# Gated mix of one-token attention and a feed-forward layer: loads of K and V in two halves, from SyncE and GpSimd

## The chip, the cores and the metric

The kernel runs on one core of a Trainium2 chip. The core has engines that work side by side: PE (TensorE) multiplies matrices, DVE (VectorE) and ACT (ScalarE) work on elements, POOL (GpSimd) and SP (SyncE) are here used to issue transfers or not at all. Sixteen DMA engines move data between HBM, the large memory, and SBUF, the core's own memory of 128 partitions. Any engine that issues a DMA puts it in a queue of its own; the same sixteen DMA engines serve all queues. Engines wait for each other through semaphores, which are counters: a DMA adds 16 when it has landed.

The metric is the device time of one execution in microseconds (us), lower being better. Each kernel is run several times.

## The reference

```python
def _A_ref(x, k_cache, v_cache, wq, wo):        # x [1,1,512], caches [1,32,65536,128]
    q = (x @ wq) as [B, H, Sq, Dh]               # 32 heads of 128
    scores = einsum("bhqd,bhkd->bhqk", q, k_cache) * (Dh ** -0.5)
    p = _softmax(scores, axis=-1)
    o = einsum("bhqk,bhkd->bhqd", p, v_cache)
    return o as [B, Sq, H * Dh] @ wo
def _B_ref(x, w_gate, w_up, w_down):             # 512 -> 1792 -> 512
    return (_silu(x @ w_gate) * (x @ w_up)) @ w_down
g = _sigmoid((x * gate_w).sum(-1, keepdims=True))
return g * a + (1 - g) * b
```

(The reshapes of q and o are told in words here.) One token attends to 65536 cached tokens in each of 32 heads. K and V are bf16: 65536 x 128 x 2 bytes, 16.8 MB each per head, 1.07 GB in all. Every byte is used once.

## The kernel before, in words

**Loads.** K and V of a head come in two halves of the tokens each, z = 0 (`a`) and z = 1 (`z`). In one half a partition holds 256 neighbouring tokens, so its piece of HBM is one run of 256 x 128 x 2 bytes = 64 KB, and the load is 8.389 MB. This is one DMA (L223 to L225). All of them are issued by SyncE, in the order written in L226 to L249: K of the next head, V of this one, in turn. The very first half of K is issued in two parts of 32 KB per partition (L228), so that work starts early. Behind the loop SyncE issues the weights wo and the last half of V in shrinking pieces (L250 to L261).

**Buffers.** `mem` has 184 KB per partition. K's two halves lie at KB 32 to 96 and 0 to 64, V's at 120 to 184 and 96 to 160. They overlap, so a load can go out when the part that it overwrites has been used, and not before. This is what SyncE's waits say: it waits for `ktdone`, which DVE counts up for each transposed eighth of a half of K, and for `pvdone`, which PE counts up four times a head in the product with V.

- the next head's first half of K is issued after four of eight transposes of this head's second half, and the second half after four transposes of the first;
- V's second half goes out after the product has used the first 40 of 64 groups of rows of V's first half, and the next head's first half after the first 40 groups of the second.

So there is never more than one load of K and one of V that has been issued and not used in part.

**Work on K.** DVE transposes K in eighths (L415 for the first half, L422 for the second; L322 for head 0) into two buffers `kt` in turn. PE multiplies each with q (`scores`, L472, 32 matmuls for an eighth) and counts `qkdone`. DVE may be no more than two eighths ahead.

**Work on V.** In head i PE also does the product of head i-1's probabilities with V (`values`, L525): `values(0, 0)` after six eighths of K's first half, `values(0, 1)` after all eight, `values(1, 0)` after the second half, `values(1, 1)` behind the maximum of the scores. Parts 0 have 40 matmuls, parts 1 have 24. PE runs this order as written; a wait of one step holds up all behind it. Before `values(0, 0)` PE waits for `d["va"]`, before `values(1, 0)` for `d["vz"]`; DVE waits for `d["ka"]` in L407 and `d["kz"]` in L418 before the transposes of a half. Each of these semaphores stands for one buffer's loads.

GpSimd writes four constants at the start and has nothing else to do.

Of the kernel before, what the change touches and what calls it, by code (L numbers as in the profile page):

```python
# [21 lines left out]
def bass_gated_mix__mha_block_cached__swiglu_ffn__decode_kernel(  # L22
# [13 lines left out]
    _, H, S, Dh = A_k_cache.shape  # L36
# [5 lines left out]
    HR = R // 2  # L42
    NP = HR // PR
# [21 lines left out]
    with ExitStack() as ctx:  # L65
# [6 lines left out]
        def sem(name):  # L72
            return ctx.enter_context(nc.semaphore(name))
# [35 lines left out]
        def at(kb, n):  # L109
            return mem[:, kb * KB:kb * KB + n]  # L110
# [9 lines left out]

        names = ("x", "gw", "wq", "wg", "wu", "wd", "ka0", "ka", "kz", "va", "vz", "wo", "wj", "w31")
        d = {n: sem("d_" + n) for n in names}
        dt_ = [sem(f"d_t{i}") for i in range(len(tail))]
        s_ones = sem("s_ones")
        s_sel0 = sem("s_sel0")
# [75 lines left out]
        def place(kind, h, z):  # L201
            if kind == "k":
                return (KA, V0)[z] if isinstance(h, int) and h == 0 else (KA, KZ)[z]
            return (VA, VZ)[z]
# [12 lines left out]
        ctx.callback(lambda: nc.sync.wait_ge(s_out2, 16))  # L217
        block = ctx.enter_context(nc.Block())

        @block.sync  # L220
        def _(sp):
            def load(kind, h, z):
                cache = A_k_cache if kind == "k" else A_v_cache  # L223
                sp.dma_start(at(place(kind, h, z), HR * Dh), kv_dram(cache, h)[z]).then_inc(d[kind + "az"[z]], 16)  # L224

            half = HR // 2 * Dh  # L226
            for n in range(2):
                sp.dma_start(at(KA + 32 * n, half), kv_dram(A_k_cache, 0)[0][:, n * half:n * half + half]).then_inc(  # L228
                    (d["ka0"], d["ka"])[n], 16)
            sp.wait_ge(s_q, 1)  # L230
            load("k", 0, 1)
            sp.wait_ge(ktdone, NP)
            load("k", 1, 0)
            sp.wait_ge(ktdone, 2 * NP - 3)
            sp.wait_ge(s_b, 1)
            load("v", 0, 0)
            sp.wait_ge(ktdone, 2 * NP + NP // 2)
            load("k", 1, 1)
            sp.wait_ge(pvdone, 5)
            load("v", 0, 1)  # L240
            with nc.sync.Fori(0, H - 2) as i:
                sp.wait_ge(ktdone, i * (2 * NP) + (4 * NP - 4))
                load("k", i + 2, 0)
                sp.wait_ge(pvdone, i * 4 + 7)
                load("v", i + 1, 0)
                sp.wait_ge(ktdone, i * (2 * NP) + (4 * NP + NP // 2))
                load("k", i + 2, 1)
                sp.wait_ge(pvdone, i * 4 + 9)
                load("v", i + 1, 1)  # L249
            sp.wait_ge(ktdone, 2 * NP * H - NP)  # L250
            sp.dma_start(at(WO, 31 * D), w_dram["wo"][:, 0:31 * D]).then_inc(d["wo"], 16)
            src = A_v_cache[0, H - 1].rearrange("(b p r) d -> b p (r d)", b=2, p=P)
            need = {0: (ktdone, 2 * NP * H - 4), 1: (ktdone, 2 * NP * H), 2: (pvdone, 4 * H - 1)}
            for n, (kb, r0, nr) in enumerate(tail):
                if n in need:
                    sp.wait_ge(*need[n])
                b, o = divmod(r0, HR)
                sp.dma_start(at(kb, nr * Dh), src[b][:, o * Dh:(o + nr) * Dh]).then_inc(dt_[n], 16)
            sp.wait_ge(pvdone, 4 * H)
            sp.dma_start(at(WOJ, D), wj_dram).then_inc(d["wj"], 16)  # L260
            sp.dma_start(at(WO31, D), w31_dram).then_inc(d["w31"], 16)  # L261
            sp.wait_ge(s_fin, 1)
            sp.dma_start(out_dram[2:4, :], fin[32:34, :]).then_inc(s_out2, 16)
# [41 lines left out]
        def _(dve):  # L305
# [6 lines left out]

            def transposes(z):
                dve.wait_ge(d[("ka0", "kz")[z]], 16)
                for c, u in enumerate(k_order[z]):
                    i = NP * z + c
                    if i == NP // 2:
                        dve.wait_ge(d["ka"], 16)
                    if i >= 2:
                        dve.wait_ge(qkdone, i - 1)  # L320
                    src = at(place("k", 0, z) + 8 * u, PR * Dh).bitcast(U32)
                    nc.vector.transpose(kt[:, i % 2, :].rearrange("p (j r t) -> p r j t", j=2, t=32),  # L322
                                        src.rearrange("p (r j t) -> p r j t", j=2, t=32)).then_inc(ktdone, 1)
# [79 lines left out]
            with nc.vector.Fori(1, H) as i:  # L403
                n = i * (2 * NP)
                v = i * 4
                dma = i * 16
                dve.wait_ge(d["ka"], dma + 16)  # L407
                for c, u in enumerate(k_order[0]):
                    if c == NP // 2:
                        dve.wait_ge(expdone, i)  # L410
                        dve.wait_ge(pvdone, v - 2)
                        shuffle(0, s_pba)
                    dve.wait_ge(qkdone, n + (c - 1))
                    src = at(KA + 8 * u, PR * Dh).bitcast(U32)
                    nc.vector.transpose(kt[:, c % 2, :].rearrange("p (j r t) -> p r j t", j=2, t=32),  # L415
                                        src.rearrange("p (r j t) -> p r j t", j=2, t=32)).then_inc(ktdone, 1)
                late(v, i, i)
                dve.wait_ge(d["kz"], dma + 16)  # L418
                for c, u in enumerate(k_order[1]):
                    dve.wait_ge(qkdone, n + (NP + c - 1))  # L420
                    src = at(KZ + 8 * u, PR * Dh).bitcast(U32)
                    nc.vector.transpose(kt[:, c % 2, :].rearrange("p (j r t) -> p r j t", j=2, t=32),  # L422
                                        src.rearrange("p (r j t) -> p r j t", j=2, t=32)).then_inc(ktdone, 1)
                top(i, n + 2 * NP)
# [20 lines left out]
        def _(pe):  # L445
# [58 lines left out]
            with nc.tensor.Fori(0, H) as i:  # L504
                n = i * (2 * NP)

                def pair(c, j):
                    for b in range(2):
                        if c == 0 and b == 0:
                            pe.wait_ge(s_qc, i + 1)  # L510
                        pe.wait_ge(ktdone, n + (c + b + 1) if j is None else n + j * 2 + (c + b + 1))
                        scores(b, PR * c, j)

                def pieces(z, c0, c1):
                    if c1 - c0 == 2:
                        pair(NP * z + c0, None)
                        return
                    with nc.tensor.Fori(0, (c1 - c0) // 2) as j:
                        pair(NP * z + c0, j)

                def values(z, part):
                    rows = v_order[z][part]
                    vt = at((VA, VZ)[z], HR * Dh)
                    for m, r in enumerate(rows):
                        last = nc.tensor.matmul(psO[0:4, :], pb[:, k_col[256 * z + r]:k_col[256 * z + r] + 4],  # L525
                                                vt[:, r * Dh:(r + 4) * Dh],
                                                start=(z == 0 and part == 0 and m == 0),
                                                stop=(z == 1 and part == 1 and m == len(rows) - 1))
                    last.then_inc(pvdone, 1)

                pieces(0, 0, NP - 2)
                with nc.tensor.If(i > 0):
                    pe.wait_ge(s_or, i)
                    pe.wait_ge(d["va"], i * 16)
                    pe.wait_ge(s_pba, i)
                    values(0, 0)
                pieces(0, NP - 2, NP)
                with nc.tensor.If(i > 0):
                    turn()
                    values(0, 1)  # L540
                pieces(1, 0, NP)
                with nc.tensor.If(i > 0):
                    pe.wait_ge(d["vz"], i * 16)
                    pe.wait_ge(s_pbz, i)
                    values(1, 0)
                pe.wait_ge(s_mx, i + 1)
                nc.tensor.matmul(mrow, mxs, ident[:], start=True, stop=True).then_inc(s_mt, 1)  # L547
                pe.wait_ge(s_gm, i + 1)
                nc.tensor.matmul(amx, onesf[0:1, :], gm, start=True, stop=True).then_inc(s_ar, 1)  # L549
                with nc.tensor.If(i > 0):  # L550
                    values(1, 1)
                pe.wait_ge(expdone, i + 1)
                nc.tensor.matmul(Lt, onesf[:], rsum, start=True, stop=True).then_inc(s_L, 1)  # L553
# [77 lines left out]
```

## Time and profile before

| | |
|---|---|
| time, median of 3 runs | 2514.06 us (2513.88 to 2514.1) |
| span of the profiled execution | 2512.4 us |
| HBM read in it | 1087.77 MB |
| PE, DVE, ACT, POOL busy | 68%, 56%, 3%, 0% of the span |
| chain that ended last | DMA 70%, PE 27% |

The profile is one execution, recorded by the hardware. "Busy" counts the time in which an engine ran an instruction; issuing a DMA isn't counted. The slices show busy time along the span in 40 equal parts of 62.8 us. The groups name line, engine and operation, then out<-in, the number of instructions, their busy time and mean, and the idle time before them with what ended it. The chain of waits goes back from the last instruction to what released it each time. For a DMA issue, "us to landing" is the time from its issue to the arrival of all its data, and it includes the time behind other loads. In the order of time, a row that merges several instructions of a line has its start, its length and their number; SPq, ACTq and the like are the engines' issuing side.

### The profile page before, as it was taken

What the parts mean: (1) busy time and instruction counts of PE and PEld (TensorE: products, weight loads), DVE (VectorE), ACT (ScalarE), POOL (GpSimd) and SP (SyncE); (2) the same over time, 40 slices, a digit from 0 to 9 for tenths busy, and PEclk for the clock granted to TensorE, in tenths of its full rate; (3) what the DMA queues carried; (4) which work ended last, traced back from release to release, by engine and by line L of the source; (5) the groups of instructions that cost most, each with busy time, mean ns of one, the idle gap of its engine ahead of it and who ended that gap; (6) DMA issues with size and microseconds to landing.
All of it is one profiled execution on the core that took longest, in us unless ns stands there. A gap on an engine that the chain in (4) does not pass through costs nothing.

```text
span 2512.4 us, 51694 instructions
## 1 busy us (share of the span) xinstructions
PE 1709.8 (68%) x21624; PEld 978.8 (39%) x21624; DVE 1411.8 (56%) x1683; ACT 64.6 (3%) x195; POOL 0.2 (0%) x4
## 2 busy tenths in 40 slices
PE   4666766667667677676676766766767767677677
PEld 3334433333433344333443333343334333344334
DVE  4764565554655645646456555465564564645653
ACT  0000000000000000000000000000000000000000
POOL 0000000000000000000000000000000000000000
PEclk8667767777677677776776767767767677677677
DMA  9999999999999999999999999999999999999999
GB/s 420 436 434 434 434 435 434 434 434 434 434 434 434 434 434 434 434 434 434 434 434 434 434 434 434 434 434 434 434 434 434 434 434 434 435 434 434 434 435 402
DMA packets 20470, 1087.93 MB, mean 433 GB/s; under 512 B 2282, under 2 KB 2668, under 8 KB 2924
## 3 DMA queue, kind: packets, MB, share of 16 engines
q1 hardware_dynamic: 20452, 1087.78, 100.0%
q8 instruction: 9, 0.15, 0.0%
q14 instruction: 1, 0.01, 0.0%
q10 hardware_dynamic: 8, 0.00, 0.0%
HBM read 1087.77 MB, written 0.00 MB: 433 GB/s over the span
## 4 chain that ended last, share of the span: by engine, by line
DMA 70%; PE 27%; DVE 1%; issue 1%; SPq 0%; ACT 0%; DVEq 0%
DMA mem<-in_A_v_cache_dram 67%; PE psO L525 27%; DMA mem<-in_A_k_cache_dram 2%; DMA mem<-in_A_wo_dram 1%; DVE kt L322 1%; DMA mem<-in_A_wq_dram 0%; DVE kt L415 0%; SPq L224 0%; PE psM L456 0%; DVE pb L331 0%; PE psS L472 0%; PE psM L547 0%; DVE sm L336 0%; PE psZ L600 0%; PE psM L549 0%
## 5 line engine op out<-in xcount | busy, mean ns | idle before, releaser
L472 PE MATMUL psS<-qcur,kt 128*128 128x4 bf16 x16384 | 573.0, 169 | 728.3 <-DVE kt L415 414.2
L525 PE MATMUL psO<-mem,pb 128*4 128x512 bf16 x3968 | 1040.6, 428 | 32.9 <-DMA mem<-in_A_v_cache_dram 32.6
L472 PEld LDWEIGHTS psS<-qcur,kt 128*128 128x128 bf16 x16384 | 534.0, 105 | 791.9 <-issue 789.5
L422 DVE STREAM_TRANSPOSE kt<-mem 128x2048 uint32<-128x2048 uint32 x248 | 547.6, 2275 | 402.3 <-DMA mem<-in_A_k_cache_dram 402.3
L415 DVE STREAM_TRANSPOSE kt<-mem 128x2048 uint32<-128x2048 uint32 x248 | 551.3, 2280 | 240.3 <-DMA mem<-in_A_k_cache_dram 239.3
L525 PEld LDWEIGHTS psO<-mem,pb 128*4 128x4 bf16 x3968 | 359.4, 93 | 657.5 <-issue 238.4
L331 DVE COPY pb<-pa 32x64 bf16<-32x64 bf16 x1024 | 233.5, 228 | 15.1 <-ACT pa L288 1.5
L338 DVE TENSOR_REDUCE sc<-psM 1x1 f32<-1x128 f32 x32 | 8.9, 279 | 334.9 <-PE psM L547 334.9
L336 DVE TENSOR_REDUCE sm<-psS 128x1 f32<-128x512 f32 x32 | 22.1, 692 | 42.3 <-PE psS L472 42.3
L322 DVE STREAM_TRANSPOSE kt<-mem 128x2048 uint32<-128x2048 uint32 x16 | 35.4, 2277 | 17.0 <-DMA mem<-in_A_k_cache_dram 17.0
L286 ACT ACTIVATE sm<-psM 128x1 f32<-128x1 f32 x32 | 5.5, 171 | 1222.7 <-PE psM L549 1222.7
L282 ACT ACTIVATE oTn<-psT,gcol 128x1 f32 (+1 forms) x31 | 8.2, 264 | 1035.1 <-PE psT L499 1035.1
L499 PE MATMUL psT<-ident,orow 4*128 4x1 f32 x256 | 33.5, 248 | 0.5 <-ACT orow L280 0.5
L499 PEld LDWEIGHTS psT<-ident,orow 4*128 4x128 f32 x256 | 30.8, 186 | 1.2 <-ACT orow L280 0.6
L280 ACT ACTIVATE orow<-psO,sm 4x512 f32<-4x512 f32 x31 | 21.0, 677 | 130.3 <-PE psO L525 126.0
L288 ACT ACTIVATE pa<-psS,sm 128x512 bf16<-128x512 f32 x32 | 22.0, 687 | 1.0
L549 PE MATMUL psM<-sc,onesf 1*128 1x1 f32 x64 | 12.3, 259 | 11.9 <-DVE sc L338 11.9
L561 PE MATMUL psW<-pb,mem 128*128 128x1 bf16 x512 | 14.5, 164 | 5.2 <-DMA mem<-in_A_v_cache_dram 4.7
L549 PEld LDWEIGHTS psM<-sc,onesf 1*128 1x128 f32 x64 | 9.6, 186 | 21.5 <-DVE sc L338 21.5
L561 PEld LDWEIGHTS psW<-pb,mem 128*128 128x128 bf16 x512 | 13.9, 100 | 6.4 <-issue 4.2
L553 PEld LDWEIGHTS psM<-sm,onesf 128*128 128x128 f32 x64 | 9.7, 191 | 14.7 <-issue 13.5
L553 PE MATMUL psM<-sm,onesf 128*128 128x1 f32 x64 | 12.5, 264 | 1.1 <-ACT pa L288 1.1
(72 smaller groups left out, 94.0 us busy)
## 6 DMA issues: line engine op xcount, KB each, us to landing
mem<-in_A_v_cache_dram SPq DMA_DIRECT2D x3, 4096.0 KB, 29.4
mem<-in_A_k_cache_dram SPq DMA_DIRECT2D x2, 4096.0 KB, 38.7
mem<-in_A_wq_dram SPq DMA_DIRECT2D x1, 4096.0 KB, 12.3
mem<-in_A_wo_dram SPq DMA_DIRECT2D x1, 3968.0 KB, 36.7
mem<-in_A_v_cache_dram SPq DMA_DIRECT2D x1, 2048.0 KB, 31.2
mem<-in_B_w_gate_dram SPq DMA_DIRECT2D x1, 1792.0 KB, 16.0
mem<-in_B_w_up_dram SPq DMA_DIRECT2D x1, 1792.0 KB, 21.0
mem<-in_B_w_down_dram SPq DMA_DIRECT2D x1, 1792.0 KB, 24.7
```

The source lines that it names most:

```text
L288: nc.scalar.activation(pa[:], psS[:], ACT.Exp, bias=nbias, scale=SCALE, accum_out=rsum).then_inc(expdone, 1)
L322: nc.vector.transpose(kt[:, i % 2, :].rearrange("p (j r t) -> p r j t", j=2, t=32), src.rearrange("p (r j t) -> p r j t", j=2, t=32)).then ...
L331: last = nc.vector.tensor_copy(dst, sr)
L336: nc.vector.reduce_max(mxs, psS[:], AX_X).then_inc(s_mx, 1)
L415: nc.vector.transpose(kt[:, c % 2, :].rearrange("p (j r t) -> p r j t", j=2, t=32), src.rearrange("p (r j t) -> p r j t", j=2, t=32)).then ...
L422: nc.vector.transpose(kt[:, c % 2, :].rearrange("p (j r t) -> p r j t", j=2, t=32), src.rearrange("p (r j t) -> p r j t", j=2, t=32)).then ...
L472: last = nc.tensor.matmul(psS[:, o:o + 4] if j is None else psS[:, ds(j * (2 * PR) + o, 4)], ktb[b][:, je // 2, r, :, je % 2], qcur[:, je, ...
L499: last = nc.tensor.matmul(psT[:, 0:1], orow[0:4, i * Dh:(i + 1) * Dh], ident[0:4, i:i + 1], start=(i == 0), stop=(i == 3))
L525: last = nc.tensor.matmul(psO[0:4, :], pb[:, k_col[256 * z + r]:k_col[256 * z + r] + 4], vt[:, r * Dh:(r + 4) * Dh], start=(z == 0 and par ...
L549: nc.tensor.matmul(amx, onesf[0:1, :], gm, start=True, stop=True).then_inc(s_ar, 1)
L553: nc.tensor.matmul(Lt, onesf[:], rsum, start=True, stop=True).then_inc(s_L, 1)
L561: last = nc.tensor.matmul(psW[:, 0:1], vt[:, r * Dh:(r + 1) * Dh], pb[:, col:col + 1], start=(r0 + r == 0), stop=(r0 + r == R - 1))
```

## The change

Each load of K and V behind the first is issued as two DMAs. A function `stream(eng, part)` holds the list of waits and loads that SyncE had, and both SyncE (part 0) and GpSimd (part 1) run it. Part 0 loads the first 32 KB of each partition's run, part 1 the second 32 KB, into the same places as before. Both wait for the same counts. GpSimd's DMAs have `single_packet=True`: the pieces that one DMA engine gets of such a DMA, eight rows of 32 KB, are marked as one packet. They add to semaphores of their own, `gl`, one for each of the four buffers, and DVE and PE wait for these too. The first half of K stays with SyncE in two parts, and so do the weights and the pieces of the last half of V.

```diff
+        gl = {n: sem("gl_" + n) for n in ("ka", "kz", "va", "vz")}
...
+        def stream(eng, part, **kw):
+            half = HR // 2 * Dh
+
+            def load(kind, h, z):
+                cache = A_k_cache if kind == "k" else A_v_cache
+                eng.dma_start(at(place(kind, h, z) + 32 * part, half),
+                              kv_dram(cache, h)[z][:, part * half:(part + 1) * half], **kw).then_inc((d, gl)[part][kind + "az"[z]], 16)
+
+            if part == 0:
+                for n in range(2):
+                    eng.dma_start(at(KA + 32 * n, half), kv_dram(A_k_cache, 0)[0][:, n * half:n * half + half]).then_inc(
+                        (d["ka0"], d["ka"])[n], 16)
+            eng.wait_ge(s_q, 1)
+            load("k", 0, 1)
...
+            with eng.Fori(0, H - 2) as i:
+                eng.wait_ge(ktdone, i * (2 * NP) + (4 * NP - 4))
+                load("k", i + 2, 0)
+                eng.wait_ge(pvdone, i * 4 + 7)
+                load("v", i + 1, 0)
+                eng.wait_ge(ktdone, i * (2 * NP) + (4 * NP + NP // 2))
+                load("k", i + 2, 1)
+                eng.wait_ge(pvdone, i * 4 + 9)
+                load("v", i + 1, 1)
+
+        @block.gpsimd
+        def _(gp):
+            stream(gp, 1, single_packet=True)
+
         @block.sync
         def _(sp):
-            def load(kind, h, z):
-                cache = A_k_cache if kind == "k" else A_v_cache
-                sp.dma_start(at(place(kind, h, z), HR * Dh), kv_dram(cache, h)[z]).then_inc(d[kind + "az"[z]], 16)
...
+            stream(sp, 0)
             sp.wait_ge(ktdone, 2 * NP * H - NP)
...
+                if z == 1:
+                    dve.wait_ge(gl["kz"], 16)
...
                 dve.wait_ge(d["ka"], dma + 16)
+                dve.wait_ge(gl["ka"], dma)
...
                 dve.wait_ge(d["kz"], dma + 16)
+                dve.wait_ge(gl["kz"], dma + 16)
...
                     pe.wait_ge(d["va"], i * 16)
+                    pe.wait_ge(gl["va"], i * 16)
...
                     pe.wait_ge(d["vz"], i * 16)
+                    pe.wait_ge(gl["vz"], i * 16)
```

More of the change, by code (lines that the diff above doesn't have):

```diff
@@ L218, in bass_gated_mix__mha_block_cached__swiglu_ffn__decode_kernel @@
         block = ctx.enter_context(nc.Block())
+        def stream(eng, part, **kw):
[10 more added lines that the diff above has]
+            load("k", 0, 1)
+            eng.wait_ge(ktdone, NP)
+            load("k", 1, 0)
+            eng.wait_ge(ktdone, 2 * NP - 3)
+            eng.wait_ge(s_b, 1)
+            load("v", 0, 0)
+            eng.wait_ge(ktdone, 2 * NP + NP // 2)
+            load("k", 1, 1)
+            eng.wait_ge(pvdone, 5)
+            load("v", 0, 1)
+            with eng.Fori(0, H - 2) as i:
[7 more added lines that the diff above has]
+                load("v", i + 1, 1)
@@ L220, in _ @@
+        @block.gpsimd
+        def _(gp):
+            stream(gp, 1, single_packet=True)
         @block.sync
         def _(sp):
-            def load(kind, h, z):
-                cache = A_k_cache if kind == "k" else A_v_cache
[L224 to L249, printed above, removed]
+            stream(sp, 0)
```

## The prediction

> **What bounds the kernel now.** I read the page's head and queues first, then the chain of waits, then SyncE's waits and the order of time of one head in the middle. The page:
>
> ```profile
> span 2512.4 us, 51694 instructions
> ...
> PE 1709.8 (68%) x21624; PEld 978.8 (39%) x21624; DVE 1411.8 (56%) x1683; ACT 64.6 (3%) x195; POOL 0.2 (0%) x4
> ...
> DMA  9999999999999999999999999999999999999999
> GB/s 420 436 434 434 434 435 434 434 434 434 434 434 434 434 434 434 434 434 434 434 434 434 434 434 434 434 434 434 434 434 434 434 434 434 435 434 434 434 435 402
> DMA packets 20470, 1087.93 MB, mean 433 GB/s; under 512 B 2282, under 2 KB 2668, under 8 KB 2924
> ...
> q1 hardware_dynamic: 20452, 1087.78, 100.0%
> ...
> L525 PE MATMUL psO<-mem,pb 128*4 128x512 bf16 x3968 | 1040.6, 428 | 32.9 <-DMA mem<-in_A_v_cache_dram 32.6
> ```
>
> All sixteen DMA engines are busy in every slice, at 434 GB/s, and SyncE's queue alone carries that. PE and DVE have room; L525, the product with V, waited 32.6 us in all for V's data. So the end is set by bytes, as long as the engines always have a load waiting. A whole load is 256 rows of 128 bf16 elements on 128 partitions, 8.389 MB, and takes 8.389 MB / 434 GB/s = 19.33 us. Four of them make a head, 77.3 us.
>
> The chain of waits (start, length, what) and SyncE's issues in the same stretch show how the queue stays full:
>
> ```profile
> 1186.16 10.97 PE psO L525 x40
> ...
> 1197.29 27.52 DMA mem<-in_A_v_cache_dram
> ...
> 1224.85 10.41 PE psO L525 x40
> ...
> 1235.43 27.96 DMA mem<-in_A_v_cache_dram
> ...
> 1263.43 11.58 PE psO L525 x40
> ...
> 1275.17 26.91 DMA mem<-in_A_v_cache_dram
> ```
>
> ```profile
> 1197.29 0.33 SPq L224 DMA_DIRECT2D mem<-in_A_v_cache_dram  x1
> 1214.61 0.33 SPq L224 DMA_DIRECT2D mem<-in_A_k_cache_dram  x1
> 1235.43 0.33 SPq L224 DMA_DIRECT2D mem<-in_A_v_cache_dram  x1
> 1253.28 0.33 SPq L224 DMA_DIRECT2D mem<-in_A_k_cache_dram  x1
> ```
>
> ```profile
> 1205.54 17.67 DVE L422 STREAM_TRANSPOSE kt<-mem 128x2048 uint32<-128x2048 uint32 x8 [13.01 <-DMA mem<-in_A_k_cache_dram]
> 1244.22 8.89 DVE L415 STREAM_TRANSPOSE kt<-mem 128x2048 uint32<-128x2048 uint32 x4 [8.44 <-DMA mem<-in_A_k_cache_dram]
> ```
>
> Two loops share the engines, one for V and one for K, each with one load out at a time. V: issued at 1197.29, landed when L525 starts at 1224.85, and the next V is issued 40 matmuls later, at 1235.43. Its time from landing to next issue is 10.58 us, in the other half 1275.17 - 1263.43 = 11.74; mean 11.16. K: landed at 1205.54, next issue at 1214.61, 9.07 us later (four transposes of L422); 1244.22 to 1253.28 is 9.06. A load waits for the one before it in line: V was issued 1205.54 - 1197.29 = 8.25 us before K had landed, K 1224.85 - 1214.61 = 10.24 us before V had landed. These 8 to 10 us are the whole reserve that keeps the engines busy. They depend on loads being served one after the other.
>
> **The change part by part.** *The issues.* GpSimd gets SyncE's list of waits and issues the upper half of every row. On POOL nothing stands before it (x4, the constants), nothing behind it. SyncE issues as many DMAs as before; only the final copies of wo and V stay on it alone. Both halves wait for the same count, so neither starts earlier than today's load. How long an issue from GpSimd takes to reach the engines no row shows. From below I take the first small load, on ScalarE's queue, from above the first large one:
>
> ```profile
> 0.74 0.54 ACTq L214 DMA_DIRECT2D mem<-in_A_x_dram  x1
> ...
> 2.15 0.26 PE L450 MATMUL psM<-ones,mem 1*128 1x1 bf16 x4 [2.15 <-DMA mem<-in_A_x_dram]
> ```
>
> ```profile
> mem<-in_A_wq_dram SPq DMA_DIRECT2D x1, 4096.0 KB, 12.3
> ...
> mem<-in_A_k_cache_dram SPq DMA_DIRECT2D x63, 29.5
> mem<-in_A_v_cache_dram SPq DMA_DIRECT2D x62, 27.5
> ```
>
> (The last two rows are the whole loads, 63 of K and 62 of V.) That is 2.15 - 0.74 = 1.4 us, and 12.3 less 9.66 (half of 19.33, for 4096 KB) = 2.6 us. I take the middle, 2.0 us, for issue and completion together. Today it is hidden in the 8.25 us.
>
> *The shorter rows.* Rows are 32 KB in place of 64 KB. The first K came in two halves with 32 KB rows, the next load in 64 KB rows:
>
> ```profile
> 36.78 8.89 DVE L322 STREAM_TRANSPOSE kt<-mem 128x2048 uint32<-128x2048 uint32 x4 [5.76 <-DMA mem<-in_A_k_cache_dram]
> 46.44 8.89 DVE L322 STREAM_TRANSPOSE kt<-mem 128x2048 uint32<-128x2048 uint32 x4 [0.77 <-DMA mem<-in_A_k_cache_dram]
> 65.83 2.31 DVE L322 STREAM_TRANSPOSE kt<-mem 128x2048 uint32<-128x2048 uint32 x1 [10.50 <-DMA mem<-in_A_k_cache_dram]
> ```
>
> A half took 46.44 - 36.78 = 9.66 us, the whole one 65.83 - 46.44 = 19.39. So two halves cost 19.32, no more than a whole; I take 0, with 0.07 us either way per load, 9 us over the 125 loads that are split.
>
> *The added waits.* DVE waits for both halves of K, PE for both of V; each costs nothing when the halves land together, and the later half counts when they don't. Behind PE's wait for V stand `pieces(0, 6, 8)`, so the scores on which DVE's next transposes wait.
>
> *The turn of the engines.* This decides. The page counts 20470 - 2924 = 17546 packets of 8 KB or more. The 125 whole loads have 125 x 128 = 16000 rows, and twelve smaller loads with rows of 8 KB or more have 12 x 128 = 1536: together 17536. So on SyncE's queue one row is one packet, and an engine gets eight of them per load. GpSimd's eight half rows of an engine are marked as one packet. With both queues filled, an engine that takes turns packet by packet moves one half row for SyncE (9.66 / 8 = 1.2 us), then GpSimd's eight (9.66 us). From one side, the mark could have no effect on turns: then half rows alternate, loads stay in order, and the part costs 0. From the other, the packet is moved in one go; then GpSimd's half of a load overtakes what is left of the load before it in SyncE's queue. I take the second: the count shows that packets are what the queue is made of, and a mark that makes eight rows one of them should count as one.
>
> [...]
>
> *What it does to the loops.* V is issued, its GpSimd packet goes (9.66 us), then its half rows on SyncE's queue start. K landed shortly before that issue (below), so the next K is issued about 7.6 us after V's (9.07 - 1.5), and 2.0 later its packet is at the engines. V's rows would need until 2.0 + 19.33 = 21.3, so K's packet goes in front of most of them. V lands late by a whole packet of K:
>
> - V's own data 19.33, K's packet 9.66, issue and completion 2.0, landing to next issue 11.16: 42.15 us per V load.
> - Today: one load of V and one of K, 2 x 19.33 = 38.66 us; V's own rows agree, (27.52 + 27.96) / 2 + 11.16 = 38.9.
> - Check: after V has landed only K's half on SyncE's queue is left, 9.66 us; V's next load reaches the engines after 11.16 + 2.0 = 13.16. So they idle 3.5 us, and K lands 11.16 - 9.66 = 1.5 us before V's issue, as used above.
>
> V's loop has become the longer one: 42.15 - 38.66 = 3.49 us for each V load. There are 62 whole V loads, so 61 steps: 61 x 3.49 = 213 us. 2512.4 + 213 = 2725. The runs' median is 1.7 us above the span (2514.06), so 2727.
>
> Bounds of this case: with 1.4 us of latency 61 x 2.89 = 176, with 2.6 us 61 x 4.09 = 249, so to 2763. If K's packet comes too late to overtake V, engines idle only between K's landing and its next issue, 9.07 + 1.4 - 9.66 = 0.8 us: 61 x 0.8 = 49, from 2563. Own range 2563 to 2765.
>
> **The rivals.** *Halves keep step (not slower).* The mark changes no turn, or the queues share evenly in some other way. For it: both halves wait on the same count, and K's and V's order is then as today; a GpSimd issue may be up to 8.25 us late before the engines run dry. Against it: the packet count. The time is today's, 2514, with 9 us either way from the shorter rows. [...]
>
> *Two queues fill gaps (faster).* If an engine begins one queue's packet while the other's ends, small pauses go. The best slice of the page has 436 GB/s against 434: 2514 x 434 / 436 = 2502. Against it: 100% busy already, and no other slice above 435.
>
> *GpSimd's issue is late (slower, by another way).* [...] It decides only from 8.25 us on: at 10 us each load loses 1.75 us, 125 x 1.75 = 219, 2733. For it: no row shows GpSimd issuing. Against it: an issue takes 0.33 us on SyncE and 0.54 on ScalarE, and POOL has nothing else to do.
>
> **How the numbers follow.** The likeliest is the overtaking packet, 0.52, 2727 us. Halves in step 0.34, gaps filled 0.05, late GpSimd 0.09. The range takes in the first two with their bounds, and room above for latencies under load: 2505 to 2790. It leaves out some of the last two, about 0.1 in all. This kernel's measurement tells about 0.2% (5 us) from no change. Faster: 0.05 and a little of the second case (0.01), 0.06. Same: 0.27 of the second case. Slower: the first and the last (0.61) and 0.06 of the second, 0.67.
>
> **What would show it.** If right: the GB/s row falls from 434 to near 434 x 38.66 / 42.15 = 398 and the DMA row shows gaps; in the chain, V's landings go from 27.5 to about 31 us; among the DMA issues GpSimd's halves land well before SyncE's. L525's idle time before V grows from 32.9 us in all. If halves keep step, the two halves' median landing times lie within 2 us of each other and the GB/s row stays at 434. If GpSimd is late, its halves land last and SyncE's wait little. What would make me wrong is above all an engine that switches within a packet, or SyncE's rows grouped into packets as large as GpSimd's.

## The result and the profile after

| | before | after |
|---|---|---|
| time, median | 2513.94 us (5 runs) | 2522.72 us (5 runs, 2522.13 to 2523.03) |
| ratio, 95% interval | | 1.0034 (1.0024 to 1.0045) |
| span of the profiled execution | 2512.4 us | 2521.1 us |

The changed kernel is slower by 8.8 us, 0.34%. The forecast was 2727 us. It was wrong by its likeliest case; the case that came is the second, halves that keep step, at the upper edge of its own bounds (2514 and 9 us either way).

The page after, with the slices, the packets and the queues:

```profile
span 2521.1 us, 52305 instructions
...
DMA  9999999999999999999999999999999999999999
GB/s 418 411 434 434 433 435 434 433 433 433 433 433 433 433 433 434 434 435 434 433 433 433 433 433 433 433 434 434 433 435 435 433 433 433 433 433 433 433 433 403
DMA packets 38470, 1087.94 MB, mean 432 GB/s; under 512 B 4282, under 2 KB 4668, under 8 KB 4924
...
q1 hardware_dynamic: 20452, 563.49, 51.8%
q0 software_dynamic: 18000, 524.30, 48.2%
...
L540 PE MATMUL psO<-mem,pb 128*4 128x512 bf16 x3968 | 1041.3, 429 | 34.0 <-DMA mem<-in_A_v_cache_dram 34.0
```

Three things are to be seen. The steady slices have 433 GB/s, 1 less than before. The second slice has 411, 25 less than before (436). And GpSimd's queue, q0, counts 18000 packets: 16000 half rows and 125 x 16 = 2000 short ones (the page has 4282 under 512 B, before 2282), taken here as the completions. So the page counts every row by itself; whether eight marked rows still move in one turn has to be read from their order.

Here is that order: the packets of each queue that begin between 1214 and 1215 us, and in the microsecond behind it (number, MB, share of the engines' time):

```profile
q1 hardware_dynamic: 14, 0.46, 106.1%
q0 software_dynamic: 1, 0.03, 7.6%
```

```profile
q0 software_dynamic: 15, 0.49, 113.7%
q1 hardware_dynamic: 1, 0.03, 7.6%
```

First nearly all sixteen engines take a half row (32 KB) of SyncE's queue, then nearly all take one of GpSimd's. A half row takes 1.2 us, so eight in one turn would keep an engine for 9.66 us, half of a load's 19.33. But between 200 and 2400 us no stretch longer than 1.64 us passes without a new half row of each queue. So a turn is one row, in spite of the mark.

The DMA issues, with the median time from issue to landing, and V's part of the chain of waits in the middle (SyncE's x65 are the split loads and a few early and late loads of the same size):

```profile
mem<-in_A_k_cache_dram SPq DMA_DIRECT2D x65, 4096.0 KB, 25.9
mem<-in_A_v_cache_dram SPq DMA_DIRECT2D x65, 4096.0 KB, 24.1
mem<-in_A_k_cache_dram POOLq DMA_DIRECT2D x63, 4096.0 KB, 29.0
mem<-in_A_v_cache_dram POOLq DMA_DIRECT2D x62, 4096.0 KB, 27.1
```

```profile
1206.07 27.04 DMA mem<-in_A_v_cache_dram
...
1233.20 10.38 PE psO L540 x40
...
1244.24 27.60 DMA mem<-in_A_v_cache_dram
```

The same V in the order of time, on SyncE's and GpSimd's issuing sides:

```profile
1205.59 0.33 SPq L226 DMA_DIRECT2D mem<-in_A_v_cache_dram  x1
```

```profile
1206.07 0.53 POOL L226 DMA_DIRECT2D mem<-in_A_v_cache_dram  x1 [20.75 <-PE psO L540]
```

GpSimd issues 0.48 us behind SyncE, and its halves land last, by about 3 us, not first. The forecast's sign for halves in step was landing within 2 us of each other, so this sign was missed by 1 us. V's step from one issue to the next, 1244.24 - 1206.07 = 38.2 us in this half, is that of before (1235.43 - 1197.29 = 38.1). L540 waits 34.0 us for V in all, where it waited 32.6.

The start is where the order did change. DVE's transposes of head 0 in order of time (before, they stood at 36.78, 46.44 and 65.83):

```profile
46.63 8.89 DVE L335 STREAM_TRANSPOSE kt<-mem 128x2048 uint32<-128x2048 uint32 x4 [13.02 <-DMA mem<-in_A_k_cache_dram]
56.28 8.89 DVE L335 STREAM_TRANSPOSE kt<-mem 128x2048 uint32<-128x2048 uint32 x4 [0.77 <-DMA mem<-in_A_k_cache_dram]
65.94 2.31 DVE L335 STREAM_TRANSPOSE kt<-mem 128x2048 uint32<-128x2048 uint32 x1 [0.76 <-DMA mem<-in_A_k_cache_dram]
```

The first half of K comes 10 us later. At 17 us SyncE's queue still holds weights and this half. GpSimd's first load, half of K's second half, goes out at 17.20 us, has a queue to itself and takes turns with them: the last of these weights, `w_down`, lands 34.6 us after its issue, before 24.7. K of head 1 waits for these transposes. Before, it was issued at 55.36 us, some 10 us ahead of the landing of the load in front. Now GpSimd's part goes out at 65.48 (SyncE's at 65.20), when that load has just landed:

```profile
65.48 0.53 POOL L226 DMA_DIRECT2D mem<-in_A_k_cache_dram  x1 [47.62 <-DVE kt L335]
```

So the engines run dry. The stretches from 60 to 90 us, before and after, and the two microseconds of the gap after, with busy times, clock, DMA share and GB/s:

```profile
60.00:90.00 30.00, 11.99 (x286) 10.65 (x287) 22.12 (x12) 1.04 (x4) 0.00 (x0) 0.50 0.99 427
```

```profile
60.00:90.00 30.00, 14.36 (x358) 12.79 (x358) 23.81 (x13) 1.04 (x4) 1.06 (x2) 0.50 0.94 397
64.00:66.00 2.00, 0.82 (x31) 0.77 (x29) 1.24 (x2) 0.00 (x0) 0.52 (x1) 0.50 0.12 45
```

(427 - 397) / 434 x 30 = 2.1 us are lost there. This is rough, since a packet's bytes count where the packet begins, and one row of 32 or 64 KB more or less on each of 16 engines is 17 or 35 GB/s in 30 us. If each packet is spread over the time that it took, the engines are idle for 2.0 us in this stretch, and before for none.

### The profile page after: what moved, and what is told of

It is laid out like the page before. It is cut to its first block, busy times and chain, and to the rows that moved or that the text cites. A ratio compares the mean times of both kernels' runs of the same rounds, so it can differ in the third digit from the quotient of the medians.

```text
span 2521.1 us, 52305 instructions
## 1 busy us (share of the span) xinstructions
PE 1711.2 (68%) x21624; PEld 980.7 (39%) x21624; DVE 1411.3 (56%) x1683; ACT 64.6 (3%) x195; POOL 67.4 (3%) x129
## 2 busy tenths in 40 slices
DMA packets 38470, 1087.94 MB, mean 432 GB/s; under 512 B 4282, under 2 KB 4668, under 8 KB 4924
## 3 DMA queue, kind: packets, MB, share of 16 engines
q1 hardware_dynamic: 20452, 563.49, 51.8%
## 4 chain that ended last, share of the span: by engine, by line
DMA 68%; PE 27%; issue 4%; POOLq 0%; DVE 0%; POOL 0%; SPq 0%; ACT 0%; DVEq 0%
DMA mem<-in_A_v_cache_dram 67%; PE psO L540 26%; DMA mem<-in_A_k_cache_dram 1%; DMA mem<-in_A_wq_dram 0%; DVE kt L429 0%; POOLq L226 0%; PE psW L578 0%; PE psM L471 0%; POOL mem L226 0%; PE psZ L617 0%; POOLq L244 0%; POOLq L249 0%; SPq L269 0%; ACT fin L311 0%; DVEq L427 0%
## 5 line engine op out<-in xcount | busy, mean ns | idle before, releaser
L540 PE MATMUL psO<-mem,pb 128*4 128x512 bf16 x3968 | 1041.3, 429 | 34.0 <-DMA mem<-in_A_v_cache_dram 34.0
L540 PEld LDWEIGHTS psO<-mem,pb 128*4 128x4 bf16 x3968 | 361.2, 93 | 657.5 <-issue 276.9
L226 POOL DMA_DIRECT2D mem<-in_A_v_cache_dram x62 | 32.7, 528 | 1272.6 <-PE psO L540 1261.3
L226 POOL DMA_DIRECT2D mem<-in_A_k_cache_dram x63 | 34.5, 547 | 1105.4 <-DVE kt L429 528.9
L566 PE MATMUL psM<-sc,onesf 1*128 1x1 f32 x64 | 12.3, 259 | 11.8 <-DVE sc L351 11.8
## 6 DMA issues: line engine op xcount, KB each, us to landing
mem<-in_A_wq_dram SPq DMA_DIRECT2D x1, 4096.0 KB, 12.3
```

The lines of the kernel that those rows point to most:

```text
L226: eng.dma_start(at(place(kind, h, z) + 32 * part, half), kv_dram(cache, h)[z][:, part * half:(part + 1) * half], **kw).then_inc((d, gl)[pa ...
```

## The experiments

The reading of the result was **theory A**: engines take turns row by row, the mark does nothing; the loss is the shorter rows, the second DMA of each load, and the start. All times below stand beside 2513.9 us for the kernel before, measured again on the same chip.

**The mark taken away.**

```diff
-            stream(gp, 1, single_packet=True)
+            stream(gp, 1)
```

> The changed kernel without the mark of one packet per engine. Theory A (the engines take turns row by row, the mark does nothing to turns): 2522.7 us as with the mark, within 1 us, GpSimd's halves landing 29.0 (K) and 27.1 us (V) after their issue as before. Rival B (the mark matters for turns or for the cost of a row): the time moves by more than 2 us, or the landing times of the two queues' halves move against each other by more than 2 us.

Measured: 2522.77 us, ratio 1.0036 (1.0023 to 1.0048). The landing times of K's halves:

```profile
mem<-in_A_k_cache_dram SPq DMA_DIRECT2D x65, 4096.0 KB, 25.9
...
mem<-in_A_k_cache_dram POOLq DMA_DIRECT2D x63, 4096.0 KB, 29.0
```

They are those with the mark. The rows of the two queues alternate here too: between 200 and 2400 us no stretch longer than 3.2 us passes without a new half row of each. For rows of 32 KB the mark changed nothing that can be seen here.

**Both halves on SyncE.**

```diff
             def load(kind, h, z):
-                eng.dma_start(at(place(kind, h, z) + 32 * part, half),
-                              kv_dram(cache, h)[z][:, part * half:(part + 1) * half], **kw).then_inc((d, gl)[part][kind + "az"[z]], 16)
+                for part in range(2):
+                    eng.dma_start(at(place(kind, h, z) + 32 * part, half),
+                                  kv_dram(cache, h)[z][:, part * half:(part + 1) * half], **kw).then_inc((d, gl)[part][kind + "az"[z]], 16)
...
-        @block.gpsimd
-        def _(gp):
-            stream(gp, 1, single_packet=True)
```

> All loads split as in the change, but SyncE issues both halves; GpSimd issues nothing. Theory A (the steady loss is the shorter rows and the second completion of each load, 5.9 us between SyncE's 15th and 131st issue in the changed kernel, 0.05 us a load): 2513.9 + 125 x 0.05 = 2520, and no gap between 60 and 70 us. Rival C (the second queue, filled by GpSimd's software, is what costs): 2514 to 2515.

Measured: 2519.46 us, 5.6 above before, ratio 1.0022 (1.0012 to 1.0032). Without GpSimd the larger part of the loss stays. Theory C fails for this part.

**The first of GpSimd's loads put back.**

```diff
             eng.wait_ge(s_q, 1)
-            load("k", 0, 1)
+            if part == 0:
+                eng.dma_start(at(place("k", 0, 1), 2 * half), kv_dram(A_k_cache, 0)[1]).then_inc(d["kz"], 16)
```

DVE's waits for `gl["kz"]` fit this (none in head 0, 16 less later).

> The changed kernel with one load put back: K of head 0, second half, is one whole DMA on SyncE's queue, so GpSimd's first load is K of head 1. Theory A (2 us are lost where GpSimd's first load overtakes the weights and the first half of K, which wait on SyncE's queue): first transposes at about 37 us as before the change, not 46.6; no gap at 60 to 70 us; 2520.5 to 2521. Rival C (cost per load of the second queue, nothing at the start): 2522.6.

Measured: 2520.54 us (1.0026, 1.0016 to 1.0036), so 2.2 us of the 8.8 were this one load. Its transposes, the stretch from 60 to 90 us and the two microseconds of the gap:

```profile
37.16 8.89 DVE L334 STREAM_TRANSPOSE kt<-mem 128x2048 uint32<-128x2048 uint32 x4 [5.76 <-DMA mem<-in_A_k_cache_dram]
```

```profile
60.00:90.00 30.00, 9.94 (x258) 8.83 (x258) 18.35 (x9) 0.00 (x0) 0.53 (x1) 0.50 0.98 418
64.00:66.00 2.00, 0.00 (x0) 0.00 (x0) 0.00 (x0) 0.00 (x0) 0.00 (x0) 0.50 0.84 352
```

As theory A said, the first half is back at 37 us, and the gap between 64 and 66 us is gone (DMA share 0.84, where it was 0.12). The stretch has 418 GB/s, where the kernel with both halves on SyncE has 436, but this difference is about one row on each engine, and with the packets spread over their time the engines are idle for 0.1 us. So it does not explain the 1.1 us by which this kernel stands above the one with both halves on SyncE. These aren't placed.

**Rows alone: one DMA for each load, cut into shorter rows.** From the kernel before, SyncE alone:

```diff
-                sp.dma_start(at(place(kind, h, z), HR * Dh), kv_dram(cache, h)[z]).then_inc(d[kind + "az"[z]], 16)
+                sp.dma_start(at(place(kind, h, z), HR * Dh), kv_dram(cache, h)[z],
+                             max_dma_last_dim=32768).then_inc(d[kind + "az"[z]], 16)
```

> The kernel before, SyncE alone, one DMA and one completion for each load, but cut into rows of 32 KB. Theory A1 (the rows are the cost): 2518 to 2519.5, near the 2519.5 of both halves on SyncE. Theory A2 (the second DMA and its completion are the cost): 2514 to 2515.

Measured: 2518.61 us, ratio 1.0019 (1.0010 to 1.0028). The same with 16384 in place of 32768:

> As the kernel with 32 KB rows, but 16 KB: three times as many rows are added to those of before. Theory A1 (a fixed time for each row): three times the loss of the 32 KB rows, about 2513.9 + 3 x 4.5 = 2527. Theory A2 (the completion is the cost): 2514 to 2515.

Measured: 2527.93 us, ratio 1.0056 (1.0041 to 1.0071). The pages' packet lines of the two:

```profile
DMA packets 36470, 1087.93 MB, mean 432 GB/s; under 512 B 2282, under 2 KB 2668, under 8 KB 2924
```

```profile
DMA packets 68470, 1087.93 MB, mean 431 GB/s; under 512 B 2282, under 2 KB 2668, under 8 KB 2924
```

16000 more packets than before cost 4.75 us, 48000 more cost 14.07. On one of 16 engines that is 4.75 / 1000 and 14.07 / 3000, 4.7 ns for each added row both times, as theory A1 said. The two DMAs of a load with their two completions are left with 2519.46 - 2518.61 = 0.85 us. The executions of these two kernels don't overlap (2518.87 is the longest of one, 2519.24 the shortest of the other), but they ran on two chips and the intervals of their ratios do overlap, so this is the least certain of the parts.

**The halves cut by partitions**, in whole rows of 64 KB:

```diff
-                eng.dma_start(at(place(kind, h, z) + 32 * part, half),
-                              kv_dram(cache, h)[z][:, part * half:(part + 1) * half], **kw).then_inc((d, gl)[part][kind + "az"[z]], 16)
+                w = slice(64 * part, 64 * part + 64)
+                eng.dma_start(at(place(kind, h, z), 2 * half)[w],
+                              kv_dram(cache, h)[z][w], **kw).then_inc((d, gl)[part][kind + "az"[z]], 16)
```

> The changed kernel with the halves cut by partitions: SyncE loads partitions 0 to 63, GpSimd 64 to 127, in whole rows of 64 KB. Theory A (shorter rows cost most of the steady loss): the row count of before is back, only the second completion and the gap at the start stay: 2515.5 to 2517.5. Rival C (the second queue costs, not the rows): 2522 to 2523.

Measured: 4842.71 us in the fastest of four executions, 4967.79 us as the median of all four. Neither theory had this. It can't tell rows from queues, which is why rows were then cut in one DMA, above. Was it the two queues? The same halves, both from SyncE:

> The halves by partitions again (0 to 63, then 64 to 127, rows of 64 KB), both issued by SyncE, so that they go through one queue. Theory H (a DMA to 64 partitions can move only at half the rate, whichever queue it is in): near the 4968 us of the two queues. Theory Q (two queues were the trouble: their rows of the two halves collide): 2514 to 2520.

Measured: 5144.84 us, ratio 2.05 (2.04 to 2.05; two executions), some per cent longer still. The slices of that page:

```profile
DMA  9999999999999999999999999999999999999999
GB/s 279 209 205 209 205 209 205 209 205 209 205 210 205 208 206 208 206 209 206 209 206 209 206 209 206 209 206 209 206 208 206 208 206 208 206 208 206 207 207 279
```

All engines are busy and move half as much, 205 to 210 GB/s for 434. A row of 64 KB took 5.1 us here and 4.9 us in the two queues, for 2.4 us before. So it is the load to 64 partitions that goes at half the rate, in one queue as in two. In the two queues both halves are out together (issued at 1226.37 and 1226.84 us in one step), and the rows are nearly as slow. The packets there show that at four of five moments at least twelve of the sixteen engines moved rows of the same half. Why these loads go at half the rate no run shows.

**K on SyncE, V on GpSimd**, whole loads, V with the mark. Each issuer keeps only its own loads and their waits, so the two lists no longer hold each other up. From the kernel before:

```diff
+            def load(kind, h, z):
+                cache = A_k_cache if kind == "k" else A_v_cache
+                eng.dma_start(at(place(kind, h, z), 2 * half), kv_dram(cache, h)[z], **kw).then_inc(d[kind + "az"[z]], 16)
...
+            eng.wait_ge(ktdone, 2 * NP - 3)
+            eng.wait_ge(s_b, 1)
+            load("v", 0, 0)
+            eng.wait_ge(pvdone, 5)
+            load("v", 0, 1)
+            with eng.Fori(0, H - 2) as i:
+                eng.wait_ge(pvdone, i * 4 + 7)
+                load("v", i + 1, 0)
+                eng.wait_ge(pvdone, i * 4 + 9)
+                load("v", i + 1, 1)
```

(Shown for V; SyncE keeps the waits and loads of K in the same way.)

> Whole loads in 64 KB rows: SyncE issues K, GpSimd issues V with the mark. Both queues hold a load at most times, so this shows what a turn is. Theory A (turns row by row, whatever the mark): K's and V's rows alternate, each load lands later than when alone in line, but the engines stay busy nearly all the time: 2514 to 2580. Theory P, the recorded forecast's (a marked DMA's eight rows go in one turn): a V load of 19.3 us goes ahead of what is left of K; by the same sums as the forecast some 11 to 13 us a head are lost, 2860 to 2915.

Measured: 2623.94 us, ratio 1.0441 (1.0425 to 1.0457). Both expectations missed, theory P by far more. V in the chain of waits:

```profile
1173.86 26.78 DMA mem<-in_A_v_cache_dram
...
1211.54 30.42 DMA mem<-in_A_v_cache_dram
...
1242.00 11.72 PE psO L537 x40
...
1254.35 26.78 DMA mem<-in_A_v_cache_dram
```

With eight rows in one turn V would land some 20 us after its issue, with its 19.33 us of data in one piece. It takes 26.8 to 30.4, so the marked rows share. But turns row by row are not free here: what is left of the load in front and the new load now share the engines, V's median from issue to landing is 29.6 us, in line 27.5 (K's is 29.5 both times), and the step is 1254.35 - 1211.54 = 42.8 us in this half. In the half before it is 1211.54 - 1173.86 = 37.7 us, no longer than before the change. The two queues' packets take 50.0% and 46.9% of the engines' time, so the engines are idle for 3.1%, or 81 of the 110 us. My sum for theory A had the latencies too small; how much of the 110 us each latency makes was not tried.

**Overtaking made in another way.** If a turn is one row, short rows on SyncE's side give GpSimd's half the larger share.

```diff
-            stream(sp, 0)
+            stream(sp, 0, max_dma_last_dim=4096)
```

> The changed kernel with SyncE's halves cut into rows of 4 KB; GpSimd's stay 32 KB. If turns go row by row, GpSimd's half of a load now gets eight times the share of SyncE's, which is the overtaking of the forecast made in another way. Theory O (the forecast's sum is right where one queue overtakes): GpSimd's halves land some 10 us before SyncE's, V's loop is the longer one, 2690 to 2780. Rival R (overtaking costs nothing, only the many rows do): 64 - 8 more rows for each of 125 loads, at the time for a row that the 32 KB and 16 KB kernels show, 2555 or less.

Measured: 2764.32 us, ratio 1.0998 (1.0981 to 1.1015). Its slices with the two queues (the last figure is the share of the engines' time), its DMA issues and its chain:

```profile
GB/s 397 402 409 386 383 404 388 406 387 387 400 389 383 407 389 399 386 387 407 384 397 392 387 407 387 383 404 389 405 389 387 399 385 389 406 390 398 387 388 402
...
q1 hardware_dynamic: 132452, 563.49, 50.6%
q0 software_dynamic: 18000, 524.30, 44.0%
```

```profile
mem<-in_A_k_cache_dram SPq DMA_DIRECT2D x65, 4096.0 KB, 29.6
mem<-in_A_v_cache_dram SPq DMA_DIRECT2D x65, 4096.0 KB, 31.7
mem<-in_A_k_cache_dram POOLq DMA_DIRECT2D x63, 4096.0 KB, 15.6
mem<-in_A_v_cache_dram POOLq DMA_DIRECT2D x62, 4096.0 KB, 15.8
```

```profile
1194.66 31.68 DMA mem<-in_A_v_cache_dram
...
1237.87 31.55 DMA mem<-in_A_v_cache_dram
...
1269.45 10.29 PE psO L540 x40
...
1279.91 31.80 DMA mem<-in_A_v_cache_dram
```

GpSimd's halves now land 14 to 16 us before SyncE's. V needs 31.6 us to land. Its step is 1279.91 - 1237.87 = 42.0 us in one half and 1237.87 - 1194.66 = 43.2 in the other, 42.6 in the mean. The forecast had 42.15 us a step and landing about 31 us, so the path is the forecast's: one queue overtakes, and V's loop becomes the longer one. Rival R would allow 2555.

Not all of the size is the forecast's, though. It had 213 us of idle engines. Here the queues take 50.6% and 44.0% of the engines' time, so the engines are idle for 5.4%, 149 us. SyncE's packets took 50.6% of 2762.8 us, against 51.8% of 2521.1 us in the changed kernel: 92 us more. At 4.7 ns for each of the 56 x 125 more rows that an engine gets it would be 33. While SyncE's short rows were alone, from 1270 to 1278 us, they moved at 420 GB/s, which is about 5 ns a row, so it is between the long rows that they took longer. Why was not tried, and that the two parts together come so near the forecast is in part luck.

And it shows the turns: between 1258 and 1260 us 32 rows of GpSimd's queue begin and 31 of SyncE's, one for one, though one is 32 KB and the other 4 KB. So with rows of 4 KB against 32 KB GpSimd's half runs ahead (by 14 to 16 us), and with rows of 32 KB against 32 KB it doesn't (it lands 3 us behind).

**All from GpSimd**, whole rows, from K of head 1 on. SyncE returns from the list after the first head's K; DVE and PE wait for one semaphore a load again:

```diff
-                eng.dma_start(at(place(kind, h, z) + 32 * part, half),
-                              kv_dram(cache, h)[z][:, part * half:(part + 1) * half], **kw).then_inc((d, gl)[part][kind + "az"[z]], 16)
+                eng.dma_start(at(place(kind, h, z), 2 * half), kv_dram(cache, h)[z], **kw).then_inc((d, gl)[part][kind + "az"[z]], 16)
...
-            eng.wait_ge(s_q, 1)
-            load("k", 0, 1)
+                eng.wait_ge(s_q, 1)
+                load("k", 0, 1)
+                return
```

> Whole loads in 64 KB rows, all from K of head 1 on issued by GpSimd with the mark; the first head's K, wo and the last half of V stay on SyncE. One queue at a time is in use but for the end. Theory A (GpSimd's queue itself is as good as SyncE's; rows, the second completion and the sharing of the engines made the loss): 2513 to 2516. Theory C (a load from GpSimd's queue is dearer): 2517 or more.

Measured: 2527.63 us, ratio 1.0053 (1.0037 to 1.0070). By the number theory C is right, by its place it isn't. The stretches of this kernel, and the last 88 us of the kernel before:

```profile
60.00:90.00 30.00, 7.91 (x217) 7.40 (x218) 16.45 (x8) 0.00 (x0) 0.53 (x1) 0.50 0.93 392
200.00:2400.00 2200.00, 1513.47 (x18661) 854.81 (x18658) 1242.66 (x1437) 55.76 (x169) 60.78 (x114) 0.72 1.00 434
2440.00:2528.00 88.00, 61.74 (x956) 37.19 (x952) 28.29 (x52) 2.41 (x7) 0.21 (x1) 0.69 0.85 362
```

```profile
2424.40:2512.40 88.00, 70.30 (x1027) 41.26 (x1024) 32.58 (x70) 2.41 (x7) 0.00 (x0) 0.75 0.96 411
```

Between 200 and 2400 us GpSimd's queue moves 434 GB/s, as SyncE's does. Most of the loss is where both queues hold loads: at the start (427 - 392) / 434 x 30 = 2.4 us, and at the end (411 - 362) / 434 x 88 = 9.9 us. With the packets spread over their time the engines are idle for 2.6 us at the start (before for none) and for 12.4 at the end (before 2.8), which agrees. Together the two are 12.3 of the 15.7 us by which this execution's span is longer (2528.1 against 2512.4 us; the runs' medians differ by 13.7). The end isn't the sharing of the queues alone. SyncE no longer stands in the list of loads, so it issues wo before the last load that GpSimd issues, V of the last head but one; before, wo came behind it (2433.85 against 2433.30). (The pieces behind wo are both halves of the last head's V.)

```profile
2430.76 0.33 SPq L262 DMA_DIRECT2D mem<-in_A_wo_dram  x1
```

```profile
2439.68 0.53 POOL L226 DMA_DIRECT2D mem<-in_A_v_cache_dram  x1 [20.45 <-PE psO L536]
```

So wo is out together with the last K and V of GpSimd's queue, and what waits for these comes late: the product with that V (L536) starts at 2481.24 us, 41.6 us behind its issue, before at 2461.26, 28.0 us behind.

## Why the prediction was wrong, point by point

- **What bounds the kernel: right.** Bytes and a queue that never runs dry. Of the loss in the changed kernel, what could be placed was a gap or time added to rows.
- **The turn of the engines: the step that failed.** The forecast took the mark to make eight rows one turn of 9.66 us, because the page's count showed one packet per row on SyncE's queue. The runs showed a turn of one row on both queues: the half rows alternate every 1.2 us, GpSimd's half lands 3 us after SyncE's instead of well before it, and the time without the mark is the same (2522.77 against 2522.72 us). So nothing is overtaken in the steady state, and of the forecast's 3.49 us for each V load nothing came. The count could not have told: the page counts each row by itself on GpSimd's queue too, 18000 with the mark and without it. I took the word in the source for a fact of the queue, though the other bound, 0, stood beside it.
- **What overtaking does to the loops: the path was right, for a case that the change does not make.** Where one queue does run ahead, V's step was 42.6 us for 42.15 forecast, its rate 383 to 409 GB/s for 398, the time 2764 us for 2727 (its own range ended at 2765). But the engines were idle for 149 us, not 213; the rest was rows that took longer, so the nearness of the sums is in part luck.
- **The second case, halves keep step: this is what came.** Its time was mis-sized within its bounds. The shorter rows were put at 0 by one pair of loads (9.66 and 19.39 us), with 9 us either way; they cost 4.75 us. An engine gets eight more rows in a load, 0.04 us at 4.7 ns, which is less than the 0.07 us by which two loads differ. That the 8.8 us lie within the 9 is luck: the bound was for the rows alone, and the other 4.1 us come from what was not in the sum.
- **The issues and the added waits.** GpSimd issued 0.48 us behind SyncE (1206.07 against 1205.59 for the same V) and that was hidden; the late issue of the last rival didn't happen.
- **The start: not in the sum.** I took GpSimd's list of waits as the same and looked no further. In head 0 only SyncE's queue has a backlog, and there a load from the other queue overtakes: the first half of K came 10 us later. It cost 2.2 us.
- **Gaps filled by two queues: not seen**, 433 GB/s against 434.

The loss step by step: rows 4.75 us, second DMA 0.85, the other queue from K of head 1 on 1.1, GpSimd's first load 2.2. These are differences between neighbouring kernels, so they add up to the whole in any case; that they do is no proof of the parts. The rows have a test of their own (the 16 KB rows), GpSimd's first load shows its gap, and the two small parts are only differences of times.

## What to carry to other kernels

Here all DMA engines were busy with one queue at 434 GB/s; a second queue added nothing (433 GB/s) and took away the order of loads. In such a kernel ask where the two queues have unequal backlogs or unequal rows, since that's where a later load overtook an earlier one here (10 us at the start, 14 to 16 us with rows of 4 KB against 32 KB). Keep rows long, since each added row cost 4.7 ns here on top of its bytes. A mark in the source is a wish (2522.77 us without it, 2522.72 with it); whether the queue honours it is read from the order of the packets and from landing times, and until then both bounds are equally open.

## What the runs showed of the hardware

- With both queues filled, the engines took one row from each in turn, of 32 KB against 32 KB (no stretch longer than 1.64 us without a new row of each) and of 4 KB against 32 KB (31 and 32 rows begun in 2 us), and a mark for one packet did not change it (2522.77 us without, 2522.72 with).
- On SyncE's queue each added row cost 4.7 ns, the same from 64 to 32 and from 64 to 16 KB. Rows of 4 KB between rows of 32 KB cost more: 92 us for 7000 more rows on each engine, about 13 ns.
- Loads to partitions 0 to 63 and 64 to 127 on one queue moved about 207 GB/s with all engines busy, half the 434 of loads to 128.
- GpSimd's queue carried 434 GB/s by itself with 64 KB rows, as much as SyncE's.
- Two queues with rows of 32 KB each shared the engines so evenly that halves issued 0.5 us apart landed about 3 us apart after 24 to 29 us, with or without the mark.
